# Measured DMA latencies, a new load order, replicas in four pieces and two rules for fillers in a list-scheduled attention and MLP kernel

## The chip, the cores and the metric

The kernel runs on one core of a Trainium2 chip. The metric is the device time of one execution in microseconds (us). Each kernel was run four times beside four to eight runs of the kernel before on the same chip, and a time given for a kernel is the median of its runs. An interval is a 95% interval of the ratio of two kernels. All profiles are of one execution, and unless it is said otherwise that execution was one of the undisturbed ("fast") ones.

## The reference, cut to what matters

```python
xn = layernorm(x)                              # x: 1 x 2048 x 512, bf16
return x + A(xn, wq, wk, wv, wo, beta) + B(xn, w1, w2)

# A: 32 heads of 16, the sequence in 4 segments of 512. For each segment s:
p     = softmax(causal(q_s @ k_s.T * scale))   # attention inside the segment
a_dot = p @ v_s
a_mem = (phi(q_s) @ M) / (phi(q_s) @ z + 1e-6) # memory of the segments before
o     = g * a_mem + (1 - g) * a_dot            # g = sigmoid(beta)
M, z  = M + phi(k_s).T @ v_s, z + sum(phi(k_s))
# B: silu(xn @ w1) @ w2, with F = 1792
```

Two reciprocals, that of the softmax's denominator and that of the memory's denominator (`den`), come out with one row for each head. They have to be multiplied with tiles in which a head takes 16 partitions. The kernel writes each reciprocal to DRAM and reads it back with every row copied to 16 partitions. Such a read is called a replica here: `R` for the softmax, `Dr` for the memory.

## The kernel before

The kernel is a program that makes a program. Every instruction is entered as a task with an engine, a duration, a time after which its result can be used (`vis`), the tasks it depends on, the buffers it takes and frees, and a rank (`due`). A list scheduler then plays through time and, for each free engine, picks the ready task of lowest rank. The order that it finds is the order of the instructions that each engine is given. When an entered latency is too short, the consumer stands too early in its engine's queue, and what stands behind it waits: in the kernel before, VectorE's eviction at 18.94 us, which was ready, came only after statistics that had waited 10.41 us for a load.

```python
def pick(e):
    c = [t for t in pool[e] if t.ready <= now + 1e-9 and can(t)]   # can: its buffers are free
    ...
    if e == "ACT":
        s = [t for t in c if t.kind == "exp"]
        if s:
            return min(s, key=lambda t: t.seq)                     # the exponential goes first
        b = min(c, key=lambda t: (t.due, t.seq))
        if st["exps"] < nexps and st["exp_next"] is not None:
            if now + b.dur > st["exp_next"] + 0.06:                # a filler may not delay it
                return None
        return b
    return min(c, key=lambda t: (t.due, t.seq))                    # VectorE, GpSimd, SP
```

A filler is any work that an engine may do between the instructions of the attention; most of it is the MLP's. An h tile is one of the 14 tiles of `silu(xn @ w1)` of a segment.

PSUM is split into one large tile `psS` for the scores and four single banks `ps`, which every other matmul shares. A bank is free again when VectorE or ScalarE has evicted it. Normalised rows `xn` go through three buffers; each is free when its transpose is done, which for segments 1 to 3 is a DMA on SP's queue.

```python
banks = Ring([pp.tile([P, L], F32, name=f"ps{i}") for i in range(NBANK)])   # NBANK = 4
xn_r = ring(3, [P, D], BF16, "xn")
fly = Ring([0] * NH_FLY)                                                    # NH_FLY = 2: h tiles in flight
...
load_x(0, 1, "SP", 0); load_x(1, 1, "ACTQ", 0); load_x(2, 1, "SP", 0); load_x(3, 1, "ACTQ", 0)
ld_k = load_w(w_k[:], kv(A_wk), "SP", 0, 5.0)
ld_q = load_w(w_q[:], kv(A_wq), "ACTQ", 0, 6.5)
ld_v = load_w(w_v[:], kv(A_wv), "SP", 0, 7.5)
ld_b = load_w(bet[:], ..., "SP", 0, 3.0)
ld_1 = load_w(w_1[:], kv(B_w1), "SP", 0.1, 10.0)       # 1.8 MB, all in front of x tiles 4 to 7
load_x(4, 4, "SP", 0.2)
...
e = A("SP", 0.5, f_d, [n], due, vis=3.0, takes=(xnT_b[s],), frees=(xb, xnT_b[s]), label="xnT")
...
def f_6():                                             # the replica: 8 rows -> 128 partitions
    nc.sync.dma_start(
        out=rb.tile[:].rearrange("p a b -> p (a b)"),
        in_=dap(dE[s], 0, [[DT * L, 8], [0, DH], [1, DT * L]]),
    )
d4 = A("SP", 0.5, f_6, [d3], due + 7, vis=3.5, takes=(rb,), frees=(rb,), label="den")
for dt in range(DT):                                   # four consumers, one for each quarter
    ... pq_ev[u] = pool(1.2, f_7, [d4], due + 10, frees=(pb, rb), label="pq")
```

The softmax here doesn't subtract the row's maximum and nothing guards it: scores larger than these inputs give would overflow.

## Time and profile before

| | before |
|---|---|
| time, median of 3 (range) | 294.89 us (294.26 to 295.34) |
| profiled execution | 298.29 us, span 296.6, slow: 1.4% above the fastest |
| PE busy, idle | 240.9 us, 55.7 us |
| mean granted TensorE clock | 0.917 |
| first matmul on w_k | 21.78 us |
| last of 80 exponentials ends | 266.3 us |

The prediction below reads the strips, waits and stretches of this profile. Two more lines of the page belong beside them. The first gives busy time and share of the span for each engine; the second says by what engine the chain of work that ended last was held.

```profile
PE 240.9 (81%) x1848; PEld 96.3 (32%) x1882; DVE 163.1 (55%) x283; ACT 194.4 (66%) x168; POOL 136.8 (46%) x201
...
PE 37%; DMA 30%; DVE 16%; POOL 5%; ACT 4%; issue 3%; SPq 3%; DVEq 0%; ACTq 0%; POOLq 0%
```

PE is the busiest engine, yet the chain that set the end ran through it for 37% of the span only, and for 30% through DMAs. In the chain itself, a replica stands with the time from its issue until it was used (start, us, step):

```profile
156.06 6.87 DMA R<-dR
192.19 6.87 DMA Dr<-dE
...
264.56 4.63 DMA R<-dR
```

The scheduler had counted on 3.5 us for each. The last one carries 384 KB, the others 512 KB.

### The profile page before, as it was taken

Reading aid. Unit: us, or ns where it says so; the run is one execution under the profiler, and the core shown is the slowest. Engines: PE = TensorE matmul, PEld = TensorE weight load, DVE = VectorE, ACT = ScalarE, POOL = GpSimd, SP = SyncE. Lnnn points to the kernel's source line nnn. Section 1 sums busy time; section 2 is a strip of 40 time slices with the busy share of each in tenths; the row PEclk is TensorE's granted clock in tenths of the full one; section 3 lists DMA queues with packets and bytes.
Section 4 is the critical chain, followed back from the end, with each engine's and each line's share of the span. In section 5 each row is a group of like instructions: output and inputs, shape, how many; then the busy total and the mean of one; then the engine's idle time right before and its main releaser. Section 6 shows DMA issues by size and latency. Waiting matters only on the chain.

```text
span 296.6 us, 4710 instructions
## 1 busy us (share of the span) xinstructions
PE 240.9 (81%) x1848; PEld 96.3 (32%) x1882; DVE 163.1 (55%) x283; ACT 194.4 (66%) x168; POOL 136.8 (46%) x201
## 2 busy tenths in 40 slices
PE   6029999999999599988695599996965799987694
PEld 6013333334333133333232133332321133333241
DVE  4056999978676755366470886421444733236600
ACT  1005898999998659969685468773789378772001
POOL 7314576664764637686239257329254123330000
PEclk9757999999999779999799589996899599999998
DMA  6899201004123022213392000130212000120001
GB/s 219 322 353 206 54 20 35 0 2 90 22 42 76 1 44 75 64 39 72 74 106 71 0 20 2 58 88 6 42 34 62 0 0 22 38 73 32 0 20 53
DMA packets 25722, 18.81 MB, mean 63 GB/s; under 512 B 15588, under 2 KB 23908, under 8 KB 25700
## 3 DMA queue, kind: packets, MB, share of 16 engines
q1 hardware_dynamic: 24884, 17.72, 24.0%
q10 hardware_dynamic: 816, 0.79, 0.9%
q8 instruction: 15, 0.25, 0.3%
q14 instruction: 7, 0.06, 0.1%
HBM read 11.73 MB, written 2.64 MB: 48 GB/s over the span
## 4 chain that ended last, share of the span: by engine, by line
PE 37%; DMA 30%; DVE 16%; POOL 5%; ACT 4%; issue 3%; SPq 3%; DVEq 0%; ACTq 0%; POOLq 0%
PE ps L463 30%; DMA R<-dR 9%; PE psS L463 7%; DMA x_all<-in_A_x_dram 6%; DMA Dr<-dE 5%; DMA dR<-Zr 3%; ACT Pt L712 3%; DVE N L957 3%; SPq L925 2%; DMA Zg<-dZ 2%; POOL Pt L726 2%; POOL pq L895 2%; DMA dD<-den 2%; DMA xnT<-xn 2%; DMA Dg<-dD 2%
## 5 line engine op out<-in xcount | busy, mean ns | idle before, releaser
L712 ACT ACTIVATE Pt<-psS 128x2048 bf16<-128x2048 f32 x80 | 150.3, 1878 | 47.8 <-PE psS L463 40.1
L726 POOL TENSOR_SCALAR_AFFINE_SELECT Pt<-Pt 128x1024 bf16<-128x1024 bf16 (+1 forms) x80 | 74.8, 935 | 86.7 <-ACT Pt L712 86.7
L463 PE MATMUL ps<-xnT,w 128*128 128x512 bf16 x211 | 58.5, 394 | 2.2 <-DVE hT L991 0.9
L463 PE MATMUL ps<-w,hT 128*128 128x512 bf16 x189 | 49.5, 393 | 3.2 <-DVE O L772 2.6
L991 DVE SCALAR_TENSOR_TENSOR hT<-hT,ps 128x512 bf16<-128x512 bf16 x56 | 37.5, 678 | 24.3 <-ACT hT L987 24.1
L987 ACT ACTIVATE hT<-ps 128x512 bf16<-128x512 f32 x56 | 32.8, 595 | 6.6 <-PE ps L463 6.6
L463 PE MATMUL ps<-Pt,V 128*32 128x128 bf16 (+3 forms) x512 | 25.6, 309 | 8.9 <-POOL Pt L726 7.7
L463 PEld LDWEIGHTS <-hT 128*128 128x128 bf16 x224 | 20.3, 99 | 35.4 <-issue 16.6
L463 PEld LDWEIGHTS <-w 128*128 128x128 bf16 x224 | 20.4, 100 | 27.2 <-issue 9.3
L463 PE MATMUL ps<-xnT,w_k 128*128 128x512 bf16 x60 | 19.6, 413 | 4.1 <-DMA xnT<-xn 2.3
L463 PE MATMUL ps<-xnT,w_q 128*128 128x512 bf16 x62 | 19.2, 409 | 3.9 <-DVE O L772 3.5
L463 PEld LDWEIGHTS <-V 128*32 128x32 bf16 x512 | 11.6, 97 | 29.4 <-issue 16.3
L463 PE MATMUL psS<-qT,kT 16*128 16x512 bf16 (+3 forms) x256 | 17.7, 308 | 3.8 <-ACT Pt L712 3.4
L895 POOL TENSOR_TENSOR pq<-pq,Dr 128x512 bf16<-128x512 bf16 x12 | 13.8, 1155 | 12.3 <-DMA Dr<-dE 12.3
L514 DVE BATCH_NORM_STATS2 st<-x_all 128x6 f32<-128x512 bf16 x16 | 10.8, 677 | 14.2 <-DMA x_all<-in_A_x_dram 14.2
L463 PE MATMUL ps<-w_v,xnT 128*128 128x512 bf16 x61 | 18.4, 406 | 0.2 <-issue 0.2
L463 PE MATMUL psS<-qT,kTo 32*128 32x256 bf16 (+3 forms) x256 | 18.1, 315 | 0.2
L772 DVE CAST N<-ps 128x512 bf16<-128x512 f32 x15 | 10.3, 685 | 13.6 <-PE ps L463 13.4
L957 DVE TENSOR_TENSOR N<-N,R 128x512 bf16<-128x512 bf16 x15 | 9.2, 664 | 14.9 <-DMA R<-dR 14.9
L772 DVE CAST O<-ps 128x512 bf16<-128x512 f32 x15 | 10.3, 684 | 11.8 <-PE ps L463 11.8
L463 PE MATMUL ps<-w_o,N 128*128 128x512 bf16 x50 | 15.3, 400 | 0.7 <-issue 0.6
L612 POOL TENSOR_SCALAR kTo<-kT,pm_odd 128x512 bf16<-128x512 bf16 x16 | 12.5, 784 | 6.1 <-DVE kT L608 6.0
(96 smaller groups left out, 233.5 us busy)
## 6 DMA issues: line engine op xcount, KB each, us to landing
w<-in_B_w_dram SPq DMA_DIRECT2D x2, 1792.0 KB
out_dram<-o_t SPq DMA_DIRECT2D x16, 128.0 KB
x_all<-in_A_x_dram SPq DMA_DIRECT2D x3, 512.0 KB
R<-dR SPq DMA_DIRECT2D x3, 512.0 KB
Dr<-dE SPq DMA_DIRECT2D x3, 512.0 KB
N<-O SPq DMA_DIRECT2D x12, 64.0 KB
w_q<-in_A_wq_dram ACTq DMA_DIRECT2D x1, 512.0 KB
w_k<-in_A_wk_dram SPq DMA_DIRECT2D x1, 512.0 KB
```

Of the source, the lines that this page charges most:

```text
L463: nc.tensor.matmul(o, lhsT=l, rhs=r, start=start, stop=stop, **k)
L514: nc.vector.bn_stats(out=b.tile[:], in_=x_all[:, t, :])
L612: nc.gpsimd.tensor_scalar(out=kTo[u].tile[:], in0=kT[u].tile[:], scalar1=pm_odd[:, 0:1], scalar2=1.0, op0=ALU.mult, op1=ALU.mult,)
L712: nc.scalar.activation(out=pb.tile[:], in_=psS[:], func=AF.Exp, scale=SCALE)
L726: nc.gpsimd.affine_select(out=v, in_=v, compare_op=ALU.is_ge, fill=0.0, base=0, pattern=pat, channel_multiplier=-1,)
L772: nc.vector.tensor_copy(out=dst.tile[:, dt, :], in_=buf.tile[:])
L895: nc.gpsimd.tensor_tensor(out=pb.tile[:], in0=pb.tile[:], in1=rb.tile[:, dt, :], op=ALU.mult)
L925: nc.sync.dma_start(out=N_b[s].tile[r, 0:nd, :], in_=O_b[s].tile[r, 0:nd, :])
L957: nc.vector.tensor_tensor(out=v, in0=v, in1=rb.tile[:, dt, :], op=ALU.mult)
L987: nc.scalar.activation(out=hb.tile[:], in_=b.tile[:], func=AF.Tanh, scale=0.5)
L991: nc.vector.scalar_tensor_tensor(out=hb.tile[:], in0=hb.tile[:], scalar=1.0, in1=b.tile[:], op0=ALU.add, op1=ALU.mult)
```

## The change

The intent: order the loads so that the first segment can start, tell the scheduler the latencies that the trace shows, let the consumers of a replica start on its first quarter, and use gaps of PE better. The diff, cut to its core:

```diff
-NH_FLY = 2
+NH_FLY = 3
+STARVE = 0.55
+LOWB = 1
@@ pick, ScalarE
-                    if now + b.dur > st["exp_next"] + 0.06:
+                    late = 0.06
+                    if not any(t.kind != "score" and t.ready <= now + 1e-9 and can(t) for t in pool["PE"]):
+                        late = STARVE
+                    if now + b.dur > st["exp_next"] + late:
                         return None
@@ pick, VectorE: the bank rule
+            if e == "DVE":
+                bk = self.names["banks"]
+                if bk.count(now) <= LOWB:
+                    f = [t for t in c if any(b.ring is bk for b in t.frees)]
+                    if f:
+                        return min(f, key=lambda t: (t.due, t.seq))
@@ loads
-    ld_1 = load_w(w_1[:], kv(B_w1), "SP", 0.1, 10.0)
-    load_x(4, 4, "SP", 0.2)
+    ld_1 = [load_w(w_1[:, :, 0:F2], kv(B_w1)[:, :, 0:F2], "SP", 0.1, 11.0)]
+    load_x(4, 2, "SP", 0.2, 12.0)
+    load_x(6, 2, "SP", 0.2, 12.5)
+    ld_1.append(load_w(w_1[:, :, F2:], kv(B_w1)[:, :, F2:], "SP", 0.3, 14.0))
     ... bet is now loaded here; x8 and x12 are entered at 22 and 23 us, w_2 at 20 ...
@@ transposes of xn and of pkT
-  A("SP", 0.5, ..., vis=3.0)
+  A("SP", 1.25, ..., vis=2.7)
@@ both replicas (the one for R alike)
-        d4 = A("SP", 0.5, f_6, [d3], due + 7, vis=3.5, ...)      # one DMA, 512 KB
         for dt in range(DT):
+            def f_6(dt=dt):
+                nc.sync.dma_start(
+                    out=rb.tile[:, dt, :],
+                    in_=dap(dE[s], dt * L, [[DT * L, 8], [0, DH], [1, L]]),
+                )
+            d4 = A("SP", 0.45, f_6, [d3], due + 7, vis=2.5, ...) # four, 128 KB each
@@ some twelve other DMA entries: 0.5/2.2 becomes 0.35 to 0.6 / 1.6 to 2.7
```

"The bank rule" is the part in VectorE's branch: with one bank left or none, VectorE does a ready task that frees a bank before any other.

More of the change, by code (lines that the diff above doesn't have):

```diff
@@ L87, in __init__ @@
         self.tasks = []
-        self.exp_left = 0
+        self.log = None
+        self.names = {}
     def add(self, eng, dur, fn, deps=(), due=0.0, vis=None, seqdeps=(), takes=(), frees=(),
@@ L153, in pick @@
                 if st["exps"] < nexps and st["exp_next"] is not None:
-                    if now + b.dur > st["exp_next"] + 0.06:
-                        return None
-                return b
+                    late = 0.06
+                    if not any(
+                        t.kind != "score" and t.ready <= now + 1e-9 and can(t) for t in pool["PE"]
+                    ):
+                        late = STARVE
+                    if now + b.dur > st["exp_next"] + late:
+                        return None
+                return b
+            if e == "DVE":
[4 more added lines that the diff above has]
+                        return min(f, key=lambda t: (t.due, t.seq))
             return min(c, key=lambda t: (t.due, t.seq))
@@ L163, in run @@
                     if t is None:
+                        if e == "PE" and self.log is not None:
+                            self.log.append((now, [
+                                (x.label, round(x.ready, 1), [n for n, r in self.names.items() for b, k in x.takes if b.ring is r and b.idx is None and r.count(now) <= k])
+                                for x in sorted(pool["PE"], key=lambda x: (x.due, x.seq))[:6]]))
                         break
@@ L259 @@
     sbank = Ring([psS])
+    sc.names.update(banks=banks, sbank=sbank)
     x_all = sb([P, NT, D], BF16, "x_all")
@@ L332, with load_x @@
     xl = {}
-    def load_x(t, n, eng, due):
+    def load_x(t, n, eng, due, vis):
         def fn():
@@ L340, in fn @@
             )
-        k = A(eng, 0.5, fn, due=due, vis=2.6 + 0.4 * n, label=f"x{t}")
+        k = A(eng, 0.5, fn, due=due, vis=vis, label=f"x{t}")
         for i in range(n):
@@ L352, in kv @@
         return w.rearrange("(ko ki) n -> ki ko n", ki=P)
-    load_x(0, 1, "SP", 0)
-    load_x(1, 1, "ACTQ", 0)
-    load_x(2, 1, "SP", 0)
-    load_x(3, 1, "ACTQ", 0)
-    ld_k = load_w(w_k[:], kv(A_wk), "SP", 0, 5.0)
-    ld_q = load_w(w_q[:], kv(A_wq), "ACTQ", 0, 6.5)
-    ld_v = load_w(w_v[:], kv(A_wv), "SP", 0, 7.5)
+    load_x(0, 1, "SP", 0, 2.85)
+    load_x(1, 1, "ACTQ", 0, 2.95)
+    load_x(2, 1, "SP", 0, 2.9)
+    load_x(3, 1, "ACTQ", 0, 3.1)
+    ld_k = load_w(w_k[:], kv(A_wk), "SP", 0, 5.6)
+    ld_q = load_w(w_q[:], kv(A_wq), "ACTQ", 0, 7.5)
+    ld_v = load_w(w_v[:], kv(A_wv), "SP", 0, 9.0)
+    F2 = F // 2
+    ld_1 = [load_w(w_1[:, :, 0:F2], kv(B_w1)[:, :, 0:F2], "SP", 0.1, 11.0)]
+    load_x(4, 2, "SP", 0.2, 12.0)
+    load_x(6, 2, "SP", 0.2, 12.5)
+    ld_1.append(load_w(w_1[:, :, F2:], kv(B_w1)[:, :, F2:], "SP", 0.3, 14.0))
     ld_b = load_w(
         bet[:], bass.AP(tensor=A_beta.tensor, offset=A_beta.offset, ap=[[0, P], [1, H]]),
-        "SP", 0, 3.0,
+        "SP", 0.35, 14.5,
     )
-    ld_1 = load_w(w_1[:], kv(B_w1), "SP", 0.1, 10.0)
-    load_x(4, 4, "SP", 0.2)
-    ld_o = load_w(w_o[:], kv(A_wo), "SP", 0.4, 14.0)
-    ld_2 = load_w(w_2[:], kv(B_w2), "SP", 0.5, 16.0)
-    load_x(8, 4, "SP", 0.6)
-    load_x(12, 4, "SP", 0.7)
+    ld_o = load_w(w_o[:], kv(A_wo), "SP", 0.4, 16.0)
+    ld_2 = load_w(w_2[:], kv(B_w2), "SP", 0.5, 20.0)
+    load_x(8, 4, "SP", 0.6, 22.0)
+    load_x(12, 4, "SP", 0.7, 23.0)
     def pool(dur, fn, deps=(), due=0.0, **k):
@@ L567, in f_d @@
                         )
-                    e = A("SP", 0.5, f_d, [n], due, vis=3.0, takes=(xnT_b[s],),
+                    e = A("SP", 1.25, f_d, [n], due, vis=2.7, takes=(xnT_b[s],),
                           frees=(xb, xnT_b[s]), label="xnT")
@@ L627, in f_t @@
                 )
-            e = A("SP", 0.5, f_t, [f], Dn(5 * u + 9), vis=3.0,
+            e = A("SP", 1.25, f_t, [f], Dn(5 * u + 9), vis=2.7,
                   takes=(phiK_b[s],), frees=(pb, phiK_b[s]), label="phiK")
@@ L732, in quad @@
                              label=f"M{n}")
+    sc.names.update(kT=kT_r, h=h_r, fly=fly)
     N_b = [Buf(N_r) for _ in range(NSEG)]
@@ L861, in f_1 @@
             )
-        d1 = A("SP", 0.5, f_1, [e], due + 2, vis=2.2, frees=(db,), label="den")
+        d1 = A("SP", 0.58, f_1, [e], due + 2, vis=2.7, frees=(db,), label="den")
         def f_2():
             nc.sync.dma_start(out=Dg[w][:], in_=dap(dD[s], 0, [[P, P], [1, P]]))
-        d2 = A("SP", 0.5, f_2, [d1], due + 3, vis=2.2, label="den")
+        d2 = A("SP", 0.4, f_2, [d1], due + 3, vis=2.0, label="den")
         def f_3():
@@ L880, in f_5 @@
             nc.sync.dma_start(out=dap(dE[s], 0, [[P, P], [1, P]]), in_=Dq[w][:])
-        d3 = A("SP", 0.5, f_5, [r2], due + 6, vis=2.2, label="den")
+        d3 = A("SP", 0.35, f_5, [r2], due + 6, vis=1.6, label="den")
         rb = Buf(Dr_r)
-        def f_6():
-            nc.sync.dma_start(
-                out=rb.tile[:].rearrange("p a b -> p (a b)"),
-                in_=dap(dE[s], 0, [[DT * L, 8], [0, DH], [1, DT * L]]),
-            )
-        d4 = A("SP", 0.5, f_6, [d3], due + 7, vis=3.5, takes=(rb,), frees=(rb,), label="den")
         for dt in range(DT):
@@ L892, in den @@
             pb = phi_q[u][0]
+            def f_6(dt=dt):
[3 more added lines that the diff above has]
+                )
+            d4 = A("SP", 0.45, f_6, [d3], due + 7, vis=2.5, takes=(rb,), frees=(rb,), label="den")
             def f_7(dt=dt, pb=pb):
@@ L914, in norm @@
             ev = [(E_ev if par == 0 else O_ev)[4 * s + d] for d in dts]
-            zs.append(A("SP", 0.5, f_1, ev, due, vis=2.2, frees=(N_b[s] if par == 0 else O_b[s],),
+            zs.append(A("SP", 0.55, f_1, ev, due, vis=2.0, frees=(N_b[s] if par == 0 else O_b[s],),
                         label="Z"))
@@ L919, in f_2 @@
             nc.sync.dma_start(out=Zg[w][0:np_, :], in_=dap(dZ[s], 0, [[P, np_], [1, P]]))
-        d2 = A("SP", 0.5, f_2, zs, due + 1, vis=2.2, label="Z")
+        d2 = A("SP", 0.45, f_2, zs, due + 1, vis=1.95, label="Z")
         mg = []
@@ L925, in f_m @@
                 nc.sync.dma_start(out=N_b[s].tile[r, 0:nd, :], in_=O_b[s].tile[r, 0:nd, :])
-            mg.append(A("SP", 0.5, f_m, [zs[0]] + [O_ev[4 * s + d] for d in dts] + [E_ev[4 * s + d] for d in dts], due + 1.5, vis=2.3,
+            mg.append(A("SP", 0.6, f_m, [zs[0]] + [O_ev[4 * s + d] for d in dts] + [E_ev[4 * s + d] for d in dts], due + 1.5, vis=2.6,
                         frees=(N_b[s], O_b[s]), label="mg"))
@@ L942, in f_5, with f_6 @@
             nc.sync.dma_start(out=dap(dR[s], 0, [[P, np_], [1, P]]), in_=Zr[w][0:np_, :])
-        d3 = A("SP", 0.5, f_5, [r2], due + 1, vis=2.2, label="Z")
+        d3 = A("SP", 0.35, f_5, [r2], due + 1, vis=1.6, label="Z")
         rb = Buf(R_r)
-        def f_6():
-            nc.sync.dma_start(
-                out=rb.tile[:, 0:nd, :].rearrange("p a b -> p (a b)"),
-                in_=dap(dR[s], 0, [[nd * L, 8], [0, DH], [1, nd * L]]),
-            )
-        d4 = A("SP", 0.5, f_6, [d3], due + 1, vis=3.5, takes=(rb,), frees=(rb,), label="Z")
         for dt in dts:
             u = 4 * s + dt
+            def f_6(dt=dt):
+                nc.sync.dma_start(
+                    out=rb.tile[:, dt, :],
+                    in_=dap(dR[s], dt * L, [[nd * L, 8], [0, DH], [1, L]]),
+                )
+            d4 = A("SP", 0.45, f_6, [d3], due + 1, vis=2.5, takes=(rb,), frees=(rb,), label="Z")
             def f_a(dt=dt):
@@ L957, in f_a @@
                 nc.vector.tensor_tensor(out=v, in0=v, in1=rb.tile[:, dt, :], op=ALU.mult)
-            a = A("DVE", 0.5, f_a, [d4] + mg, due_rep, frees=(rb, N_b[s]), label="a_t")
+            a = A("DVE", 0.55, f_a, [d4] + mg, due_rep, frees=(rb, N_b[s]), label="a_t")
             if s == 0:
@@ L980, in h_tile @@
         b, g = gemm4(due, lambda ki: w_1[:, ki, ft * P : (ft + 1) * P],
-                     lambda ki: xnT_b[s].tile[:, ki, :], xnT_done[s] + [ld_1], keep=1,
+                     lambda ki: xnT_b[s].tile[:, ki, :], xnT_done[s] + [ld_1[ft * P >= F2], ld_1[(ft * P + P) > F2]], keep=1,
                      takes=(fb, hb), label=f"h{s}.{ft}")
@@ L1030, in f_d @@
             nc.sync.dma_start(out=out_flat[t * P : (t + 1) * P, :], in_=ob.tile[:])
-        A("SP", 0.5, f_d, [e], due + 6, frees=(ob,), label="out")
+        A("SP", 0.35, f_d, [e], due + 6, frees=(ob,), label="out")
     def tail():
@@ L1124, in f_d @@
                     nc.sync.dma_start(out=out_flat[t * P : (t + 1) * P, :], in_=ob.tile[:])
-                A("SP", 0.5, f_d, [e], 0, frees=(ob,), label="out")
+                A("SP", 0.35, f_d, [e], 0, vis=1.75, frees=(ob,), label="out")
     ln(0, -4)
```

## The prediction

> **What bounds the kernel now.** I read the strips of the page first, then the waits by engine, then the timeline around each long wait. In the strips each column is a fortieth of the span, 7.4 us.
>
> ```profile
> PE   6029999999999599988695599996965799987694
> PEclk9757999999999779999799589996899599999998
> ```
>
> PE is the engine to keep fed: 240.9 us busy of 296.6. It has a hole at 10 to 20 us and shallower ones at about 100, 145, 160, 200 and 230; at most of them its granted clock is low too. The waits name the releasers (engine, line, releaser: total us, times, longest):
>
> ```profile
> DVE st L514 <- DMA x_all<-in_A_x_dram: 14.2, 2, 10.4
> DVE N L957 <- DMA R<-dR: 14.9, 4, 6.8
> POOL pq L895 <- DMA Dr<-dE: 12.3, 3, 5.8
> PE ps L463 <- DVE O L772: 7.8, 4, 3.5
> PE ps L463 <- POOL Pt L726: 7.7, 7, 2.9
> ```
>
> So VectorE and GpSimd stand still for loads and for the two replica transfers (R and Dr, one row copied to 16 partitions), and PE then waits for what stands behind them. The timeline shows the first case:
>
> ```profile
> 18.11 0.69 DVE L514 BATCH_NORM_STATS2 st<-x_all 128x6 f32<-128x512 bf16 x1 [10.41 <-DMA x_all<-in_A_x_dram]
> 18.94 0.66 DVE L558 CAST xnT<-ps 128x512 bf16<-128x512 f32 x1
> 21.78 0.58 PE L463 MATMUL ps<-xnT,w_k 128*128 128x512 bf16 x1 [0.77 <-DVE xnT L558]
> ```
>
> The statistics of x tile 4, which segment 0 does not need, stand in VectorE's queue ahead of the eviction (L558) that segment 0 does need. The load of tiles 4 to 7 is queued behind all of w1 and lands at 18.1. Everything starts at 21.78. The second case, at 160 us:
>
> ```profile
> 162.95 2.75 DVE L957 TENSOR_TENSOR N<-N,R 128x512 bf16<-128x512 bf16 x4 [6.79 <-DMA R<-dR]
> 166.35 1.01 PE L463 MATMUL ps<-xnT,w_q 128*128 128x512 bf16 x2 [3.52 <-DVE O L772]
> 168.02 1.88 ACT L712 ACTIVATE Pt<-psS 128x2048 bf16<-128x2048 f32 x1 [4.15 <-PE psS L463]
> ```
>
> VectorE waits 6.79 us for R, so the four PSUM banks stay full, PE waits 3.52 and the exponential stream 4.15.
>
> [...] 0.50 from 12 to 24 us and from 162 to 172. [...] the ready eviction at 18.94 waited behind the statistics. [...] a DMA share of 0.51 while Dr moves (columns: stretch, length, PE, PEld, DVE, ACT, POOL busy, clock, DMA share, GB/s):
>
> ```profile
> 118.00:119.00 1.00, 1.00 (x6) 0.48 (x5) 0.64 (x2) 1.00 (x1) 0.32 (x1) 1.00 0.51 160
> 120.00:121.00 1.00, 1.00 (x12) 0.35 (x14) 0.44 (x1) 1.00 (x1) 0.40 (x1) 1.00 0.51 118
> ```
>
> [...] I expect no more bandwidth from the split, only an earlier first quarter.
>
> **The change part by part.** No arithmetic is added or removed. The scheduler, which fixes each engine's order at build time, gets other latencies and two more rules, so the instruction order changes. I compared the built orders.
>
> *Loads.* In the new order VectorE does xn, eviction, xn, xn, eviction, kT, V, pkT, V and only then the statistics of tile 4. Before, the second reciprocal root ended at 8.25. From the start of the last xn pair (19.51) to the first w_k matmul (21.78) took 2.27 us, so the first matmul should come at 8.25 + 2.27 = 10.5. Are the weights there? The windows give 217 GB/s over the first 10 us, 2.2 MB, against 2.1 MB for four x tiles, wk, wq and wv; bet, behind wv, was seen at 12.08. wk and wq have 1.6 MB ahead of their end, about 8 us[...]: just in time. The next in line, at 350 GB/s: half of w1 (0.92 MB) complete by 12, x4-5 by 13, x6-7 by 13.6, the other half by 16. The entered latencies (11 to 14 us after issue) say much the same, so I expect no long load wait. Gain: 21.8 - 10.5 = **11.3 us**. It should survive to the end: from 30 to 90 us PE was 9.0 to 9.9 us busy of every 10, nothing there to absorb it.
>
> *Replica latency.* Before, the scheduler assumed 3.5 us; the chain shows 6.87, 6.91, 6.87 and 6.98 for 512 KB, 3.4 us late each time. Of 6.87 us some 4.4 is data (share 0.5 from about 92 to 96.5), so about 2.5 is fixed. My estimate for 128 KB: 2.5 + 1.1 = 3.6 us for the first piece at most, the rest 0.8 to 1.1 us apart, the last at 5.5 to 6.9. The new entry is 2.5 us at 0.45 us spacing, that is 2.5 to 3.85. So it is still optimistic, by about 1 us for the first piece and 2 to 3 for the last, but pieces are used one by one.
>
> *VectorE at R.* The first a_t can run about 1.0 (GpSimd scale) + 1.45 (dR) + 3.4 = 5.8 us after the Zf reciprocal. New order, at 0.68 us an operation: first R, 8 operations (5.4 us) ahead, two a_t, three others, two a_t: wait about 0.5, before 2.6. Second R, 7 ahead (4.8): about 1.5; before 6.79[...]. Third R, 5 ahead (3.4): about 2.5, before 4.29. Together 13.7 to about 4.5. The fourth is in the tail.
>
> *GpSimd at Dr.* Waits 2.1, 4.34 and 5.83. The first piece comes 3.3 us earlier and each multiplication takes 1.15 us, as long as the next piece needs. Masks stand between as before, so I expect about 2 us each, 6 in all against 12.3.
>
> *What the waits cost.* PE gaps behind R: 2.56 + 3.52 + 2.30 + 1.39 = 9.8 us. Behind Dr: 1.13 + 2.87 + 0.86 + 1.76 = 6.6 us. Then half clock. Weighting (1 - clock) by PE busy in 2 us windows, I get about 3.0 us lost at 100 to 108, 3.1 at 162 to 172, 2.8 at 202 to 210, 2.7 at 230 to 238: 11.6. Together 28 us. VectorE's waits fall to a third and GpSimd's to a half, but buffers and half clock do not follow linearly; I take 45% off: **12.6 us**.
>
> *Second filler and bank rule.* One more h tile in flight, a filler that may delay an exponential by up to 0.55 us when PE has nothing else, and VectorE first freeing banks when one or none is free. They aim at PE <- hT (4.2 us in 4 waits); 2.3 of that was behind R, already counted. A third tile also holds a third of four banks. I give it zero.
>
> *New costs.* SP issues 20 more DMAs for the replicas (7 become 27), about 0.65 us each, 13 us on an engine that mostly waits. Transposes for segment 1 now follow loads still draining until about 26 us on the same queue, and xn has three buffers: I add **1.5 us**.
>
> Sum: 294.9 - 11.3 - 12.6 + 1.5 = 272.5; I say **272**.
>
> **The rivals.** (A) Only the start is won, because the last piece still lands at 6.9 and the optimistic 2.5 us packs consumers earlier: R and Dr waits stay near 27 us and the time is about 283. For it: [...] unchanged bytes. Against: one a_t or multiplication needs only its own quarter. (B) The stalls go almost wholly: pieces land near 2.5, PE never falls to half clock, 28 us are won: 294.9 - 11.3 - 28 + 1.5 = 257. For it: 384 KB took 4.63, at 174 GB/s, so smaller pieces may move faster. Against: PE. Busy 240.9 less 11.6 clock, less 6.6 before the start, leaves 223; begun at 10.5 and with the 9 us of idleness since 270, this gives 242 even without any other gap, so 257 would need under 15 us of idleness and half clock in all. (C) The start gain is lost at a new wait, on w1, on transposes behind loads, or on bet, now behind w1: gates come late and GpSimd blocks. Then about 280. Against: in the new order the instruction that needs bet stands after the second mask, which can end no earlier than about 21 us, and bet has 4.5 MB to go before it lands, about 16 us at the rates above[...].
>
> **Range and chances.** Between A and B: 263 to 284. For slower, the 11 us of the start would have to be lost again, and no such wait is in sight. Faster by over 2% (below 289): 0.96; same 0.03; slower 0.01.
>
> **What would show it.** The first w_k matmul at 10 to 11 us; no VectorE wait over 2 us on x; R waits near 5 us and Dr waits near 6; first replica piece landing 3 to 3.6 us after issue, DMA share still 0.5; fewer half-clock stretches; the last exponential near 243 where it ended at 266.3. I am wrong if the start gain shows but the last exponential moves by only 11 us (A)[...], or if PE waits over 3 us on a load.

What no trace or run shows is cut from this text, and each cut is marked. The readings are measured: 0.50 is the granted TensorE clock, the eviction at 18.94 us stood behind statistics that had waited 10.41 us, and 0.51 is the DMA share while Dr moved. The 350 GB/s are what the DMAs of the kernel before moved from 16 to 24 us (348 to 350). The fixed 2.5 us are an estimate from one replica, 6.87 us less the 4.4 in which its data moved. That the split brings no more bandwidth, and that the second R would wait 1.5 us only, were estimates. That half clock does not follow the waits linearly was not shown at that time; e2 shows it below.

## The result

The changed kernel takes 260.96 us (median of 4, 258.82 to 265.54); the kernel before took 295.12 beside it. The ratio of fast runs is 0.882, interval 0.876 to 0.888. Such a ratio is the mean time of one kernel's fast runs over that of the other's of the same rounds, so it is not quite the ratio of the two medians. The prediction was 272 with a range of 263 to 284: the direction was right, and 11 us more were won than predicted, which is 2 us beyond the range's low end.

The page of the changed kernel (its two strips, the engines' busy time, the chain's shares):

```profile
PE 229.5 (89%) x1848; PEld 93.9 (36%) x1882; DVE 166.1 (64%) x283; ACT 193.1 (75%) x168; POOL 137.3 (53%) x201
...
PE   7599999999899779999699999999984999969774
...
PEclk9889999999999999999999999999999999979999
...
PE 46%; DVE 17%; ACT 14%; DMA 13%; issue 4%; POOL 4%; SPq 1%; ACTq 0%; DVEq 0%; POOLq 0%
```

The hole at 10 to 20 us is gone, DMAs hold 13% of the chain instead of 30%, and after the start one stretch alone has a low clock, at 230 us. The waits that answer to those in the prediction:

```profile
DVE N L980 <- DMA R<-dR: 8.3, 8, 3.7
...
POOL pq L918 <- DMA Dr<-dE: 4.3, 2, 3.8
DVE st L536 <- DMA x_all<-in_A_x_dram: 3.7, 1, 3.7
...
PE ps L485 <- POOL Pt L748: 2.3, 2, 2.1
```

(Total, times and longest, in us.) R went from 14.9 us to 8.3, of which 4.4 belong to the fourth R near the end; Dr from 12.3 to 4.3, x from 14.2 to 3.7 (what is left is the very first load). The last exponential ends at 235.1 us, where it ended at 266.3. "PE ps <- DVE O", 7.8 us before, is no longer in PE's list at all. The timeline shows the start on PE and then VectorE at the first replica:

```profile
10.89 1.37 PE L485 MATMUL ps<-xnT,w_k 128*128 128x512 bf16 x3 [0.67 <-ACT xnT L578]
...
85.90 0.43 DVE L980 TENSOR_TENSOR N<-N,R 128x512 bf16<-128x512 bf16 x1 [2.01 <-DMA R<-dR]
86.99 0.42 DVE L980 TENSOR_TENSOR N<-N,R 128x512 bf16<-128x512 bf16 x1 [0.66 <-DMA R<-dR]
87.33 0.68 DVE L630 CAST kT<-ps 128x512 bf16<-128x512 f32 x1
87.93 0.68 DVE L795 CAST O<-ps 128x512 bf16<-128x512 f32 x1
88.53 0.68 DVE L667 CAST qT<-ps 128x512 bf16<-128x512 f32 x1
89.13 1.29 DVE L980 TENSOR_TENSOR N<-N,R 128x512 bf16<-128x512 bf16 x2
```

Two quarters of R are used as they land, then three evictions free three banks, and the other two quarters follow without a wait. In the kernel before all four multiplications stood together, and the evictions stood behind them.

Where the time came from, as busy and idle time of PE. The row on the clock is an estimate by the prediction's method, (1 - clock) times PE's busy time in stretches of 2 us, for all of them after 24 us:

| | before | after |
|---|---|---|
| span of the profiled execution | 296.6 | 259.0 |
| PE idle before 30 us (gaps that the timeline shows) | 15.3 | 4.8 |
| PE idle after 30 us (same) | 34.9 | 19.3 |
| lost to half clock after 24 us | 13.6 | 1.7 |
| PE busy | 240.9 | 229.5 |

So some 10.5 us came from the start, 15.6 from gaps later, and 11.9 from the clock: 38.0 by these sums, where the two spans differ by 37.6 (the two executions were a slow one and a fast one, so a few of these are not the change's).

### The profile page after: what moved, and what is told of

Read it like the earlier page. It is cut to its first block, busy times and chain, and to the rows that moved or that the text cites. A ratio compares the mean times of both kernels' runs of the same rounds, so it can differ in the third digit from the quotient of the medians.

```text
span 259.0 us, 4745 instructions
## 1 busy us (share of the span) xinstructions
PE 229.5 (89%) x1848; PEld 93.9 (36%) x1882; DVE 166.1 (64%) x283; ACT 193.1 (75%) x168; POOL 137.3 (53%) x201
## 4 chain that ended last, share of the span: by engine, by line
PE 46%; DVE 17%; ACT 14%; DMA 13%; issue 4%; POOL 4%; SPq 1%; ACTq 0%; DVEq 0%; POOLq 0%
PE ps L485 37%; ACT Pt L734 10%; PE psS L485 9%; ACT hT L1010 3%; DMA phiK<-pkT 3%; DMA R<-dR 2%; DMA dR<-Zr 2%; DVE hT L1014 2%; DVE st L536 2%; POOL Pt L748 2%; DVE xn L554 1%; DVE pq L614 1%; DMA dE<-Dq 1%; DMA dD<-den 1%; DVE kT L630 1%
## 5 line engine op out<-in xcount | busy, mean ns | idle before, releaser
L485 PE MATMUL ps<-xnT,w 128*128 128x512 bf16 x212 | 55.6, 381 | 0.4
L485 PE MATMUL ps<-w,hT 128*128 128x512 bf16 x183 | 47.2, 385 | 1.2 <-issue 0.8
L1014 DVE SCALAR_TENSOR_TENSOR hT<-hT,ps 128x512 bf16<-128x512 bf16 x56 | 36.4, 677 | 11.7 <-ACT hT L1010 11.2
L485 PEld LDWEIGHTS <-w 128*128 128x128 bf16 x224 | 19.3, 97 | 25.3 <-issue 7.6
L485 PE MATMUL ps<-Pt,V 128*32 128x128 bf16 (+3 forms) x512 | 24.4, 307 | 4.6 <-POOL Pt L748 2.3
L1046 DVE SCALAR_TENSOR_TENSOR o_t<-ps,x_all 128x512 bf16<-128x512 f32 x12 | 8.3, 688 | 21.2 <-PE ps L485 21.2
L485 PE MATMUL ps<-xnT,w_k 128*128 128x512 bf16 x60 | 18.1, 387 | 2.2 <-DVE hT L1014 1.0
L485 PEld LDWEIGHTS <-V 128*32 128x32 bf16 x512 | 11.1, 97 | 23.1 <-issue 8.9
L634 POOL TENSOR_SCALAR kTo<-kT,pm_odd 128x512 bf16<-128x512 bf16 x16 | 12.6, 785 | 11.5 <-DVE kT L630 11.5
L485 PE MATMUL ps<-w_v,xnT 128*128 128x512 bf16 x61 | 16.7, 390 | 0.4 <-issue 0.2
L614 DVE SCALAR_TENSOR_TENSOR pq<-qT,pq 128x512 bf16<-128x512 bf16 x12 | 12.0, 997 | 4.3 <-POOL pq L608 4.3
L485 PEld LDWEIGHTS <-kT 16*128 16x128 bf16 x256 | 5.9, 91 | 22.4 <-issue 22.1
```

The lines of the kernel that those rows point to most:

```text
L485: nc.tensor.matmul(o, lhsT=l, rhs=r, start=start, stop=stop, **k)
L614: nc.vector.scalar_tensor_tensor(out=dst_b.tile[:], in0=src_b.tile[:], scalar=0.0, in1=dst_b.tile[:], op0=ALU.max, op1=ALU.add, accum_out=acc,
L634: nc.gpsimd.tensor_scalar(out=kTo[u].tile[:], in0=kT[u].tile[:], scalar1=pm_odd[:, 0:1], scalar2=1.0, op0=ALU.mult, op1=ALU.mult,)
L1014: nc.vector.scalar_tensor_tensor(out=hb.tile[:], in0=hb.tile[:], scalar=1.0, in1=b.tile[:], op0=ALU.add, op1=ALU.mult)
L1046: nc.vector.scalar_tensor_tensor(out=ob.tile[:], in0=b.tile[:], scalar=0.5, in1=x_all[:, t, :], op0=ALU.mult, op1=ALU.add,)
```

## The experiments

The parts of the diff are called loads (order, halves of w1, latencies of loads), replicas (four DMAs at 2.5 us), fillers (third h tile, late exponential, bank rule) and other latencies. All runs were correct. In each, "ratio" is against the kernel before. Its median was 296.1 in the first call (e1 to e4), 293.6 in the second (e5 to e7 and the first control), 291.4 in the third (e8, e9, the second control, e16), 293.9 in the last two.

### Each part alone

**e1: the kernel before with the loads alone.**

```diff
-    ld_1 = load_w(w_1[:], kv(B_w1), "SP", 0.1, 10.0)
-    load_x(4, 4, "SP", 0.2)
+    ld_1 = [load_w(w_1[:, :, 0:F2], ...)]; load_x(4, 2, ...); load_x(6, 2, ...); ld_1.append(load_w(w_1[:, :, F2:], ...))
```

> The kernel before with the load order, the halves of w1 and the load latencies alone. My prediction's term: 11.3 us off about 295, so 284, with the first w_k matmul near 10.9 us, and the R and Dr waits as before (near 15 and 12 us). Rival (the start gain grows downstream because the schedule is rearranged too): 277 or less.

Measured: 297.51 us (295.66 to 299.40), ratio 1.012 (1.001 to 1.023). Nothing was won, although the first w_k matmul came at 10.67 us, 11.1 earlier. The timeline of SP's queue, of VectorE and of PE shows where it went (SPq is SP issuing a DMA):

```profile
12.80 8.82 SPq L337 DMA_DIRECT2D x_all<-in_A_x_dram  x2
...
24.61 6.70 SPq L567 DMA_TRANSPOSE xnT<-xn  x4
...
29.68 0.41 DVE L535 TENSOR_SCALAR xn<-x_all,mv,rstd 128x512 bf16<-128x512 bf16 x1 [6.81 <-DMA xnT<-xn]
...
30.75 1.26 PE L466 MATMUL ps<-Pt,V 128*32 128x512 bf16 x16 [6.48 <-DVE V L665]
```

SP spent 8.8 us on issuing the last two loads. The trace does not name the reason; in the changed kernel, where the same two loads took 8.76 us to issue, the DMA share was 0.95 to 1.08 from 12 to 22 us. The transposes of segment 1 stand behind those loads. The fourth xn of the segment needs one of three buffers, all waiting for a transpose, and stands at the head of VectorE's queue. Behind it stand evictions, so the banks fill and PE waits 6.48 us. That is more than half of the 11.1 us; where the rest went is not shown.

**e2: the replicas alone.**

```diff
-        d4 = A("SP", 0.5, f_6, [d3], due + 7, vis=3.5, ...)     # 512 KB
+            d4 = A("SP", 0.45, f_6, [d3], due + 7, vis=2.5, ...) # for each dt, 128 KB
```

> The kernel before with only the replicas R and Dr split into four DMAs, entered at 2.5 us each. Theory A (the R and Dr stalls and the half clock behind them were worth most of 28 us and nearly all of it goes): 295 down to about 273 to 277. My prediction's size (45% of 28 us): about 282 to 284. Theory B (the filler and bank rules do the rest): 283 or more.

Measured: 275.78 us (274.69 to 276.98), ratio 0.938 (0.927 to 0.948). That is about 18.5 us, more than the 12.6 that I had given to this part. VectorE's wait for R fell to 3.0 us and GpSimd's for Dr to 5.6. By the method of the table above, 2.8 us were lost to half clock after the start, where it was 13.6.

**e3: the fillers alone.**

```diff
-NH_FLY = 2
+NH_FLY = 3
+STARVE = 0.55
+LOWB = 1     # with the two rules in pick, as in the change
```

> The kernel before with only the second filler: three h tiles in flight, an exponential delayed by up to 0.55 us when PE has nothing ready, VectorE freeing banks first. My prediction and theory A: no change, 293 to 297. Theory B: 285 to 288.

Measured: 280.64 us (279.35 to 281.30), ratio 0.954 (0.946 to 0.962). The part that I set to zero was worth about 14 us in the kernel before, with the waits for R and Dr still there (9.4 and 10.0 us).

**e7: the other latencies alone.**

```diff
-  A("SP", 0.5, ..., vis=3.0)      # transposes; and some twelve entries alike
+  A("SP", 1.25, ..., vis=2.7)
```

> The kernel before with the other latencies alone (transposes, den, Z, merges, outputs). They change by at most 0.75 us each, so I expect 290 to 298; a rival that puts the gain on accurate latencies in general expects below 287.

Measured: 295.24 us (294.92 to 299.49), ratio 1.010 (1.000 to 1.020): nothing.

### Each part taken out of the changed kernel

**e4: the changed kernel without the fillers.** The diff is e3's, reversed.

> The changed kernel without the filler and bank rules. Theory A: within 2 us of the changed kernel, 259 to 263. Theory B (I was wrong to count them as zero): 267 to 272.

Measured: 273.09 us (270.94 to 276.47), ratio 0.926 (0.915 to 0.938). This is about 1 us from my prediction's 272, for a kernel without the part that I had called worthless. The agreement is in part luck: the replicas were worth more than I counted (e2), and the start kept less (PE has a gap of 3.52 us at 29 us in e4's profile, quoted under e13).

**e5: the changed kernel without the four replica DMAs.** The diff is e2's, reversed.

> The changed kernel with R and Dr as one DMA each again, entered at 3.5 us as before; all else changed. If the split is worth in the end state what it is worth alone (about 20 us): 278 to 282, with R and Dr waits of 3 us each and half clock back. If filler and latencies make it superfluous: 261 to 265.

Measured: 279.52 us (275.79 to 283.15), ratio 0.951 (0.929 to 0.972). The waits are back, and the clock lost 7.2 us after the start:

```profile
POOL pq L918 <- DMA Dr<-dE: 12.4, 3, 6.4
...
DVE N L980 <- DMA R<-dR: 11.3, 3, 4.5
```

**e6: the changed kernel without the loads.** The diff is e1's, reversed.

> The changed kernel with the old loads. Loads alone gained nothing because segment 1's transposes waited behind loads and stopped VectorE for 6.8 us. My prediction's 11.3 us for the start would give about 272 here. Rival (the start is worth nothing in the end state either): 259 to 263.

Measured: 273.58 us (272.89 to 274.09), ratio 0.936 (0.929 to 0.943). VectorE waits 14.3 us for x again, longest 10.6. Here the loads are worth 12.6 us, by themselves they were worth none.

Against the changed kernel's 260.96 the three removals (replicas, fillers, loads) cost 18.6, 12.1 and 12.6 us, 43.3 in all, where the change won 34.2 (medians from different calls; the kernel before differs by up to 1.6% between them). So the parts overlap: a wait that holds PE's banks can be mended at two places.

### How much an order counts by chance

A tiny change of any entered duration makes another order. Two controls measure what that is worth: the assumed latency of a matmul goes from 0.25 to 0.26 us, in the kernel before and in the changed one.

```diff
-PE_LAT = 0.25
+PE_LAT = 0.26
```

> A control: the kernel before with one scheduler constant, the assumed time from a matmul's end to its reader, 0.26 instead of 0.25 us. Nothing real changes, but the instruction order does. If single-part differences of 10 us and more mean something: 291 to 299. If any new order gains or loses as much (chance order): outside 285 to 303.

Measured in the kernel before: 302.41 us (299.18 to 303.04), ratio 1.033 (1.021 to 1.045).

> A second control: the changed kernel with the assumed matmul latency 0.26 instead of 0.25 us. The same step moved the kernel before by about 8 us (302 against 294). If the changed kernel's order is a typical one: 257 to 267. If 261 was a lucky order: 268 or more.

Measured in the changed kernel: 263.76 us (261.84 to 266.36), ratio 0.903 (0.897 to 0.909), against 260.96 without it.

So an order found by chance moves the kernel before by 9 us and the changed one by 3. The second control ran on a chip where the kernel before took 291.4; by the ratios (0.903 against 0.882) it is 2.1%, some 6 us. One such control each is no distribution, but differences below 10 us between two orders of the kernel before, or of a few in the changed one, cannot be given to a part by the time alone. Of the readings above, 14 and 18.5 us exceed this; for the loads alone the trace shows a wait that ate most of the gain, and chance may have its share in the 0.

### The replicas: the split, or the honest entry?

**e8: the changed kernel with one DMA for each replica, entered at its measured latency.**

```diff
-            d4 = A("SP", 0.45, f_6, [d3], due + 7, vis=2.5, ...)  # four, for each dt
+        d4 = A("SP", 0.65, f_6, [d3], due + 7, vis=6.9, ...)      # one, as before the change
```

> The changed kernel with R and Dr as one DMA each, but entered at the measured 6.9 us instead of 3.5. If only an honest latency matters: as the changed kernel, 258 to 265. If the split itself matters, because the first quarter arrives about 4 us sooner: 270 or more. Undoing the split at 3.5 us gave 279.5.

Measured: 260.41 us (259.12 to 261.56), ratio 0.894 (0.890 to 0.897), the same as the changed kernel by its time (by its ratio 1.3% longer, within what the control allows) and 19 us less than e5, which differs in the entries alone. With the latency entered as it is, other work stands in front of the multiplications, and the waits are shorter than with four pieces:

```profile
DVE N L980 <- DMA R<-dR: 2.4, 2, 1.4
...
POOL pq L918 <- DMA Dr<-dE: 0.5, 1, 0.5
```

**e9: the changed kernel with the four pieces entered as they land** (about 2.95 us for the first, 0.92 more for each next).

```diff
-            d4 = A("SP", 0.45, f_6, [d3], due + 7, vis=2.5, ...)
+            d4 = A("SP", 0.62, f_6, [d3], due + 7, vis=2.95 + 0.3 * dt, ...)
```

> The changed kernel with the four pieces entered as measured, 2.95 us for the first and 0.92 us more for each next. If remaining R and Dr waits (8.3 and 4.3 us) still cost: 256 to 259. If they are hidden anyway: 259 to 265, chance order included.

Measured: 260.90 us (257.91 to 263.88), ratio 0.890 (0.883 to 0.897). No further gain.

**e17: the kernel before with the honest entry as its only change.**

```diff
-        d4 = A("SP", 0.5, f_6, [d3], due + 7, vis=3.5, ...)
+        d4 = A("SP", 0.65, f_6, [d3], due + 7, vis=6.9, ...)
```

> The kernel before with one DMA for each replica as it was, and only the latency that the scheduler counts on set to the measured 6.9 us (and 0.65 us of issue). Theory: the gain of the replicas is this entry and not the split: 272 to 279, as the four small DMAs alone gave 275.8. Rival: the earlier first quarter is needed in this kernel: 285 to 295.

Measured: 282.11 us (280.80 to 283.80), ratio 0.960 (0.953 to 0.968). This lies between both expectations: the entry alone gives some 12 us of the 18.5 that the four pieces gave in e2. VectorE's wait for R is 3.9 us and GpSimd's for Dr 0.3, so the waits did go; the gain itself is little more than the 9 us of the control. The 6 us between e17 and e2 could be the earlier first quarter or chance order, which moved this same kernel by 9 us; no run here separates them. In the end state e8 shows that the split is not needed.

### Where the start's gain is kept

**e16: e1 with five xn buffers in place of three.**

```diff
-    xn_r = ring(3, [P, D], BF16, "xn")
+    xn_r = ring(5, [P, D], BF16, "xn")
```

> The loads alone again, with five xn buffers instead of three, so that the fourth xn of segment 1 has a free buffer and VectorE does not wait for a transpose queued behind the loads. If that wait (6.8 us on VectorE, 6.5 on PE) is where the start gain went: no xn wait over 2 us before 35 us, and 285 to 291 instead of 297.5. If the gain is lost further on: 294 to 300.

Measured: 286.47 us (284.90 to 287.71), ratio 0.983 (0.978 to 0.987). The wait that e1 showed was a buffer's: with two more buffers VectorE's waits for a transpose went from 10.9 us to 0.7. The time is about 5 us below the kernel before, and the last exponential starts at 249.1 us; since the control moved this kernel by 9 us, those 5 us are not shown to be the buffers'. The rest of the start's gain did not come through, and the clock still lost 11.5 us later in that profile.

The changed kernel has three buffers all the same. Its transposes are as late as e1's (SP is done with the same two loads at 21.8 us), but VectorE's order at that place is another:

```profile
27.99 0.69 DVE L630 CAST kT<-ps 128x512 bf16<-128x512 f32 x1
28.59 0.68 DVE L667 CAST qT<-ps 128x512 bf16<-128x512 f32 x1
29.19 0.68 DVE L630 CAST kT<-ps 128x512 bf16<-128x512 f32 x1
29.79 1.58 DVE L554 TENSOR_SCALAR xn<-x_all,mv,rstd 128x512 bf16<-128x512 bf16 x2
```

It evicts until 29.8, and when xn's turn comes the buffer is free. The next three runs tell which of the fillers did it.

### Which of the three fillers

**e13: the changed kernel without the bank rule.**

```diff
-LOWB = 1
+LOWB = -1
```

> The changed kernel without the rule that lets VectorE free a bank before its other work when one bank is left. If this rule is the 12 us: 270 to 275, with more idle time of PE in front of matmuls that wait for a bank. If it is not: 259 to 265 (the chance order moves this kernel by about 3 us).

Measured: 275.06 us (271.89 to 278.71), ratio 0.931 (0.922 to 0.940). It is the 12 us, and 14 by this run. The profiled execution was a slow one (278.71; the fast ones took 271.89 to 275.12), so I read the places of its gaps from it, not its total. VectorE and PE at the two long gaps:

```profile
29.58 0.41 DVE L554 TENSOR_SCALAR xn<-x_all,mv,rstd 128x512 bf16<-128x512 bf16 x1 [5.30 <-DMA xnT<-xn]
29.91 0.68 DVE L667 CAST qT<-ps 128x512 bf16<-128x512 f32 x1
...
30.65 0.58 PE L485 MATMUL ps<-xnT,w_q 128*128 128x512 bf16 x1 [4.59 <-DVE qT L667]
...
99.32 1.43 DVE L980 TENSOR_TENSOR N<-N,R 128x512 bf16<-128x512 bf16 x2 [0.42 <-DMA R<-dR]
100.67 0.68 DVE L795 CAST O<-ps 128x512 bf16<-128x512 f32 x1
...
101.40 1.87 PE L485 MATMUL ps<-xnT,w_k 128*128 128x512 bf16 x4 [4.75 <-DVE O L795]
```

Both are one pattern. A VectorE instruction that waits for a DMA (xn for a transpose, then the multiplications with R for the replica) stands in front of an eviction that is ready, the banks stay full, and PE stops for 4.6 and 4.75 us. With the rule the evictions go first. What follows each gap is seen in the stretches (stretch, length, PE, PEld, DVE, ACT, POOL busy, clock, DMA share, GB/s):

```profile
28.00:30.00 2.00, 0.00 (x0) 0.00 (x0) 0.42 (x2) 0.00 (x0) 0.00 (x0) 0.71 1.00 198
...
32.00:34.00 2.00, 2.00 (x23) 0.70 (x16) 1.83 (x5) 0.89 (x1) 0.69 (x1) 0.50 0.00 0
...
102.00:104.00 2.00, 2.00 (x5) 0.45 (x3) 1.84 (x4) 0.00 (x0) 0.69 (x1) 0.50 0.49 167
```

From 28 to 30 us the DMA share is 1.00 while all compute engines but a little of VectorE stand idle; from 32 to 34 PE is busy throughout at a clock of 0.50, and again from 102 to 104. Half clock after the start cost 9.7 us in this profile against 1.7 in the changed kernel's. e4's profile, of a fast execution, has the first of the two gaps at the same place (3.52 us on PE at 29.19, behind an xn that waits 4.23).

**e14: the changed kernel with two h tiles in flight.**

```diff
-NH_FLY = 3
+NH_FLY = 2
```

> The changed kernel with two h tiles in flight instead of three. If the third tile is the 12 us: 270 to 275. If it is not: 259 to 265.

Measured: 261.10 us (259.82 to 262.67), ratio 0.887 (0.880 to 0.895): the third tile is worth nothing here.

**e15: the changed kernel with the old limit for a late exponential.**

```diff
-STARVE = 0.55
+STARVE = 0.06
```

> The changed kernel with the old limit of 0.06 us by which a second filler may make an exponential late, instead of 0.55 us. If this is the 12 us: 270 to 275. If it is not: 259 to 265. If the three parts share it, all three of these runs lie between 264 and 269.

Measured: 256.34 us (255.22 to 256.78), ratio 0.870 (0.865 to 0.876): outside both expectations, on the good side. Without this rule the kernel is 4 to 5 us faster, and the control moved it by 3 us, or 6 by the ratios, so I call this the fastest order found and not a proof that the rule does harm.

**e10: the bank rule alone in the kernel before.** The diff is the six lines of the rule with LOWB = 1 and some bookkeeping; the limit for a late exponential stays at 0.06.

> The kernel before with the bank rule as its only change. Theory: the rule takes away the time in which matmuls wait for a bank whose eviction stands behind other VectorE work, whatever else is changed, and is most of what second filler, third tile and rule won together (280.6): 278 to 285. Rival: in the kernel before those evictions stand behind multiplies that wait for replicas, which only honest latencies mend: 289 to 298.

Measured: 284.16 us (283.59 to 285.63), ratio 0.968 (0.961 to 0.974). So about 10 us of the 14 of all three fillers, in a kernel in which no latency was mended; by itself this is hardly more than the control's 9 us, but the waits changed with it. PE's waits for evictions of O and hT, 7.8 and 4.2 us before, are 2.3 and 3.8; the waits for R went from 14.9 to 6.3 since other work now stands in front. What is left is Dr: GpSimd's wait there is still 10.5, and PE waits 8.9 for the masks behind it, at which no VectorE rule can help.

**e18: the fastest combination that the runs pointed to**, the old limit of e15 with five xn buffers.

```diff
-STARVE = 0.55
+STARVE = 0.06
-    xn_r = ring(3, [P, D], BF16, "xn")
+    xn_r = ring(5, [P, D], BF16, "xn")
```

> The changed kernel with the old limit of 0.06 us for a late exponential and five xn buffers in place of three. If the two gains are separate, and the xn wait still costs something: 250 to 255. If the bank rule has already taken away what five buffers mend: 255 to 259, as with the old limit alone (256.3).

Measured: 257.61 us (256.60 to 258.50), ratio 0.878 (0.872 to 0.883): not better than e15. That is the second expectation: the bank rule had already mended what the two buffers mend. The best kernel is e15, with 256.34 us.

## Why the prediction was right or wrong

**The start: right in size, wrong in why it lasts.** The first w_k matmul came at 10.89 us where I said 10.5, and in the changed kernel the loads are worth 12.6 us (e6) where I said 11.3. But I argued that the gain survives because PE had no idle time to absorb it. Alone it did not survive (e1, 297.51). My rival C named the place, transposes behind loads, and I gave it too little weight; I was saved by the bank rule.

**Replicas: right in the waits, too small in what they cost.** I said 4.5 us for the first three R, and they took 3.9; 6 for Dr, and it took 4.3. The sum for R is luck: one by one I said 0.5, 1.5 and 2.5, and they were 2.67, 0.57 and 0.65. The first piece of the first R was used 2.94 us after its issue (82.96 to 85.90 us; 3.6 at most, I said), the next 1.09 later, at a DMA share of 0.45 to 0.50 from 85 to 87 us. The term that I mis-sized is "I take 45% off", 12.6 us: taking this part out costs 18.6 (e5), alone it wins as much (e2). By the count of half clock, that was the reason: of my 12.6, 7.4 were for gaps and 5.2 for half clock. In e2 half clock after the start fell from 13.6 us to 2.8, that is by 10.8, which leaves 7.7 of the 18.5 for gaps. In the changed kernel it is 1.7. It does not go in proportion to the waits: in e2 those for R and Dr together fell from 27.2 us to 8.6, to 32%, and half clock to 21%. I had also misread one stretch: the clock fell at 161.9 us (0.94 on average from 161 to 162, 0.50 from 162 to 163), before the gap of 3.52 us (162.8 to 166.4) and after one of 2.87 us in which PE waited for masks that stand behind Dr, so that half clock began before PE's stop behind R. Between 30 and 230 us PE had five gaps over 2.2 us before; after, the longest two are 2.08 us at 125.17, which was not followed by half clock (1.00 from 122 to 132 us), and 2.13 at 229.54, which was (0.50 from 230 to 233); no run shows what made the difference.

**Second filler and bank rule: the step that failed.** "They aim at PE <- hT ... I give it zero." Taken out they cost 12.1 us (e4), and the kernel without them takes 273.09, my number for the whole. The runs put it to one of the three: the bank rule, 14 us (e13), while the third h tile is worth nothing (e14), nor does it cost anything by holding a bank as I had feared, and the late exponential is worth nothing or less (e15). I had read the rule by the wait that its author would have seen, PE <- hT. What it does is wider: when banks run short in the scheduler's time, the ready evictions stand in front of whatever VectorE would wait for. I had myself described the damage, "so the four PSUM banks stay full", and had not asked which part of the change deals with that.

**New costs: not there in the end.** I added 1.5 us for transposes behind loads and three buffers. Without the bank rule they are the 4.6 us gap of e13; with it, two more buffers win nothing (e18 against e15).

**The rivals.** A (only the start won, 283) and C (280) did not come true for the whole change, though C did for the loads alone. B (257) was nearest, and e15 reached it. I had held against B that it would need under 15 us of idleness and half clock beyond what I counted. By the same count the changed kernel has about 18: PE's idle time after the first w_k matmul is about 25 us, less the 9 of the tail that I had counted, and 1.7 of half clock.

**The range.** It did not allow for chance order, 3 to 9 us in the two controls, nor for a part being worth anything that I had set to zero.

What stays open: whether the earlier first quarter is worth something when nothing else is changed (e2 against e17), and how much of e15's 4 to 5 us is the rule and how much chance.

## What to carry to other kernels

In a statically ordered kernel, look at what stands behind an instruction that waits for a DMA: if it is an eviction, a late DMA can become a stop of PE and then a stretch at half clock (in e13 stops of 4.59 and 4.75 us, and a clock of 0.50 after each). Two cures were worth 10 us and more each here: entering the latency that the trace shows (12 us in e17, 19 from e5 to e8) and letting evictions go first when banks run out (10 in e10, 14 in e13). The bank rule also kept the start's gain, which the loads alone lost. When a part of a change looks worthless by the one wait it seems to aim at, ask which other waits it would have shortened before setting it to zero, and measure how far a chance reordering moves the time before giving small differences to a cause.

## What the traces show of half clock and of DMA times

- The length of a gap of PE alone does not tell whether half clock follows. After the gap of 2.56 us in the kernel before (it ends at 101.33) the clock was 0.50 from 102 to 106 us, after that of 2.13 us in the changed kernel 0.50 from 230 to 233, and after one of 1.70 us in e16 0.50 from 74 to 75. A gap of 2.08 us in the changed kernel passed at 1.00. What decides is not shown. The gap in the timeline of e16, and the first whole stretch at half clock after it:

```profile
72.33 0.81 PE L466 MATMUL ps<-xnT,w_k 128*128 128x512 bf16 x3 [1.70 <-DMA xnT<-xn]
```

```profile
74.00:75.00 1.00, 1.00 (x4) 0.23 (x2) 0.00 (x0) 0.00 (x0) 0.00 (x0) 0.50 0.67 103
```

- A replica of 512 KB from SP was used 6.87 us after its issue (R at 156.06 us in the kernel before), the first piece of 128 KB after 2.94 (R) and 3.12 (Dr, 116.52 to 119.64) in the changed kernel.
- SP needed 8.8 us to issue two loads behind those of the weights, and the transposes issued after them were used at 29.7 us only (e1). The four pieces of R at 82.96 us in the changed kernel, where the DMA share was 0.00 to 0.01 just before, took 2.53 us to issue, about 0.6 each.
